# Attention and an MLP mixer on one core: which engine takes the partial sums and the Newton steps, and where the first large block's squares and the weight conversion stand

## The chip, the cores and the metric

The kernel runs on one core of one Trainium2 chip. The metric is the device time of one execution in microseconds. A core has five engines with their own instruction streams: TensorE (PE in the profile, PEld for its weight loads), VectorE (DVE), ScalarE (ACT), GpSimd (POOL) and SyncE (SP), which here issues nearly all DMAs. [...]

## The reference

```python
def _attn_ref(q, k, v, g_q, g_k):               # batch 8, heads 12, seq 448, head_dim 64
    def rmsnorm(x, g):
        rms = np.sqrt(np.mean(x * x, axis=-1, keepdims=True) + 1e-06)
        return x / rms * g
    q_n, k_n = (rmsnorm(q, g_q), rmsnorm(k, g_k))
    scores = 1.0 / np.sqrt(q.shape[-1]) * np.matmul(q_n, k_n.transpose(0, 1, 3, 2))
    scores = scores - np.max(scores, axis=-1, keepdims=True)
    attn = np.exp(scores)
    attn = attn / (np.sum(attn, axis=-1, keepdims=True) + 1e-09)
    return np.matmul(attn, v)
# then, with the heads side by side as x of shape (8, 448, 768):
def _moe_ref(x, w_tok1, w_tok2, w_ch1, w_ch2):  # 448x256, 256x448, 768x1536, 1536x768
    h = np.maximum(x.transpose(0, 2, 1) @ w_tok1, 0.0) @ w_tok2
    u = x + h.transpose(0, 2, 1)
    return u + np.maximum(u @ w_ch1, 0.0) @ w_ch2
```

The mixer's weights arrive as 64-bit floats (an array of 32-bit floats times a 64-bit scalar); everything else is 32-bit.

## The kernel before

**The work.** The 8 images ("b") have 12 heads each. Two heads make a pair (p, 48 in all), and two pairs make a step (t, 24 in all). Attention runs one image ahead of the mixer: while the mixer works on image b, attention works on image b + 1.

**Attention of a step.** For a pair, `square` (ACT, L1259 and L1262) and `reduce` (DVE, L1276) make the sums of squares of q and k; `roots` makes the inverse roots from them by `fold` (ACT, L1284), `guess` (DVE, L1293 and L1298) and three calls of `newton`. A Newton step is three small DVE instructions (L1317 to L1319), or four on GpSimd (L1306 to L1309) for pairs 2 to 11. Roots are made for two pairs at once, under the even pair's number. `scale` (DVE, L349) applies them, and `turn_qk` transposes q and k (from pair 12 on on DVE, L364, with ACT's scaling behind it, L367).

The keys are cut into NK = 7 chunks of 64. `score(t, k)` is 8 matmuls (L387) into two PSUM banks and two exponentials on ACT (L391) into a tile e; `values` multiplies e by v into o_ps (L461). From step 3 on the denominators are made in two stages. `group_sums(t, k)` for k = 1 to 6 adds the seven e tiles into one tile es (L429, 128 x 896): on GpSimd for k = 1 and 2, on DVE for the rest. es is a single buffer. `row_sums` sums es over its rows on PE (d_ps, L441). `denominators` takes the reciprocal of d_ps on DVE (L490, L492, L504) and scales o_ps into uT (L507), which frees the o_ps bank; ps_O has two banks, ps_S (scores and d_ps) four, ps_M (m_ps) two.

**Order.** The order on every engine is the order of emission, and two planners set it. Up to step 8, `att_step` gives four small items per step, and `merge` interleaves them with the mixer's items by their costs. From step BIG = 9 on, `big_step` gives two large blocks per step. It returns what stands ahead of the block, the block, what stands beside it, and what is spread over the units that follow (`place`; for t = 9, which is in the time of image 1's mixer, `merge`). The first block, `first_block`, has the scores 0 and 1, two or three chunks of values of the step before, its row sums and score 2. While step t is computed, the pairs n = 2t + 2 and n + 1 are made ready: for t = 9 these are pairs 20 and 21. Their q and k come by eight DMAs each on SP (L1243).

**The mixer.** For images 1 to 7 the two channel products are computed by a scheme of 7 products of half-size blocks (`ch1`, L880; `ch2`, L937) with sums around them on DVE, ACT and GpSimd (L885 to L919, L946). Image 0 instead uses 36 plain products (`first_stage`, L852), and in its time the weights are converted from 64 to 32 bits, one chunk of 128 x 512 per product. `weight_items` does for item i: the load of chunk i + 2 (SP, L176, two DMAs), the last bit operation of chunk i - 2 (DVE, L281), the first three of chunk i (DVE, L263, L264, L266), ACT's part of chunk i - 1 (L274), the last multiplication of chunk i - 2 into a stage tile (DVE, L308), and the store of chunk i - 3 (SP, L192). `first_items` puts item 19 + k behind product `begins(k)`. With that, the stage tile of product 13 + k is made in the item behind product k + 7 for k from 10 on. The sums of the weights that the 7-product scheme needs are made on GpSimd (L204 to L207); they pass through device memory and are sent from SP (L211) and loaded again (L221, L240, L811).

From image 1 on, the transposed attention output x goes through device memory too: DVE transposes (L742), SP stores (L710) and loads (L717), and then the first token product reads it (L756). The second token product (L764) is added to uT by DVE (L769).

## Time and profile before

| | |
|---|---|
| median of 3 runs | 1330.02 us (1329.81 to 1331.51) |
| the profiled execution | 1331.61 us |
| its span, first to last instruction | 1329.6 us |
| mean granted PE clock | 0.985 |
| PE busy | 1272.4 us (96%) |
| DVE busy | 767.0 us (58%) |
| ACT busy | 372.0 us (28%) |
| POOL busy | 381.0 us (29%) |
| L429 on POOL, 128 x 896 | 42 instructions, 2.09 us median |
| L429 on DVE, 128 x 896 | 84 instructions, 1.09 us median |
| L1317, L1318, L1319 on DVE, 128 x 56 | 54 each, 387, 242 and 241 ns mean |
| L1306 to L1309 on POOL, 112 x 32 | 15 each, 370, 280, 294 and 284 ns mean |

The profile cuts the span into 40 slices of 33.2 us and gives each engine's busy share in a slice in tenths (9 is 90% or more). The list of waits has: engine and line, what it waited for, total us, how often, the longest. The chain of work that ended last goes back from the last instruction, at each step to what released it; its rows are start, duration, what. An idle engine costs nothing unless the chain runs through what it does next. A list of instructions in order of time has start, duration, engine, line, and in brackets the idle time before. Image 0's mixer runs from about 100 to 274 us, image 1's to 448 us, and each later one takes 152 us.

### The profile page before, as it was taken

The page shows a single profiled execution, that of the slowest core. Times are in us where ns is not written, and L with a number is a line of the kernel's source. Part 1 is how long each engine was busy: PE and PEld are TensorE (multiplying, and loading weights), DVE is VectorE, ACT ScalarE, POOL GpSimd, SP SyncE. Part 2 cuts the span into 40 slices and gives each one's busy share as a digit, 9 for nine tenths or more (in the row PEclk, how much of TensorE's full clock was granted, in tenths as well). Part 3 has the DMA queues.
Part 4 walks back from the last instruction along what each step waited for, and adds up shares of the span by engine and source line. Part 5 has one row for each costly group of instructions (what it writes and reads, how often), then busy time and mean ns, then how long its engine had stood idle before and what let it go on. Part 6 is the DMA issues. An engine that isn't in the chain of part 4 may idle for free.

```text
span 1329.6 us, 20169 instructions
## 1 busy us (share of the span) xinstructions
PE 1272.4 (96%) x7408; PEld 936.3 (70%) x7408; DVE 767.0 (58%) x1289; ACT 372.0 (28%) x740; POOL 381.0 (29%) x449
## 2 busy tenths in 40 slices
PE   5989999889997999999999999999999999999997
PEld 3344444346776777896788868886887867797997
DVE  6887689736673366654756367554656457433212
ACT  5553333222331043302332033311433024200100
POOL 1211531255663132221242023321232123311220
PEclk9999999899998999999999999999999999999999
DMA  9656477889879766595757867585766855386554
GB/s 208 170 150 172 115 212 208 195 232 230 229 195 229 156 148 168 142 237 105 168 152 165 207 137 171 141 216 112 185 155 158 223 117 141 113 220 139 175 171 94
DMA packets 502448, 228.05 MB, mean 172 GB/s; under 512 B 374532, under 2 KB 464004, under 8 KB 502340
## 3 DMA queue, kind: packets, MB, share of 16 engines
q1 hardware_dynamic: 489218, 224.83, 68.5%
q10 hardware_dynamic: 12994, 1.84, 0.8%
q8 instruction: 61, 1.00, 0.3%
q14 instruction: 47, 0.39, 0.1%
q0 software_dynamic: 128, 0.00, 0.0%
HBM read 187.07 MB, written 39.52 MB: 170 GB/s over the span
## 4 chain that ended last, share of the span: by engine, by line
PE 82%; DVE 8%; DMA 4%; issue 2%; POOL 1%; SPq 1%; ACT 1%; DVEq 0%; POOLq 0%; ACTq 0%
PE m_ps L880 25%; PE m_ps L937 25%; PE s_ps L387 9%; PE o_ps L461 8%; PE m_ps L764 5%; PE m_ps L756 5%; PE m_ps L852 2%; DMA raw<-in_moe_w_ch_dram 1%; PE d_ps L441 1%; DVE raw L264 1%; DVE raw L281 1%; DVE stage L308 1%; DVE cv_sb L263 1%; PE t_ps L361 1%; DVE ms L1276 1%
## 5 line engine op out<-in xcount | busy, mean ns | idle before, releaser
L937 PE MATMUL m_ps<-hb,unit 128*128 128x224 f32 x1764 | 339.9, 354 | 4.2 <-issue 4.2
L937 PEld LDWEIGHTS m_ps<-hb,unit 128*128 128x128 f32 x1764 | 332.8, 190 | 15.7 <-issue 10.1
L880 PE MATMUL m_ps<-tu,unit 128*128 128x224 f32 x1008 | 201.6, 355 | 0.0
L880 PEld LDWEIGHTS m_ps<-tu,unit 128*128 128x128 f32 x1008 | 189.1, 190 | 14.1 <-issue 7.8
L391 ACT ACTIVATE e<-s_ps 128x448 f32<-128x448 f32 x294 | 138.5, 549 | 175.6 <-PE s_ps L387 173.7
L387 PE MATMUL s_ps<-qkT 64*64 64x448 f32 x1260 | 147.6, 553 | 9.2 <-ACT qkT L367 5.0
L880 PE MATMUL m_ps<-uT,unit 128*128 128x224 f32 x756 | 150.7, 353 | 0.0
L880 PEld LDWEIGHTS m_ps<-uT,unit 128*128 128x128 f32 x756 | 142.6, 190 | 5.0 <-issue 4.3
L461 PE MATMUL o_ps<-e,v 64*64 64x448 f32 x1148 | 131.3, 545 | 0.1
L946 POOL TENSOR_TENSOR uT<-uT,r 128x448 f32<-128x448 f32 (+1 forms) x56 | 49.6, 896 | 256.3 <-DVE r L946 135.5
L885 DVE TENSOR_TENSOR r<-m_ps,r 128x448 f32<-128x448 f32 x63 | 39.2, 622 | 125.3 <-POOL r L885 67.0
L387 PEld LDWEIGHTS s_ps<-qkT 64*64 64x64 f32 x1260 | 46.6, 134 | 77.8 <-issue 59.9
L946 DVE TENSOR_TENSOR uT<-uT,m_ps 128x448 f32<-128x448 f32 (+1 forms) x70 | 33.8, 499 | 108.8 <-PE m_ps L937 105.5
L461 PEld LDWEIGHTS o_ps<-e,v 64*64 64x64 f32 x1148 | 46.7, 135 | 62.8 <-issue 58.3
L429 DVE TENSOR_TENSOR es<-es,e 128x896 f32<-128x896 f32 x72 | 83.9, 1165 | 10.6 <-ACT e L391 8.0
L756 PE MATMUL m_ps<-x,w_sb 112*128 112x384 f32 x256 | 84.8, 488 | 1.0 <-ACT x L736 1.0
L885 POOL TENSOR_TENSOR hb<-r,r 128x448 f32<-128x448 f32 x21 | 24.0, 1141 | 205.3 <-ACT r L901 205.3
L764 PE MATMUL m_ps<-w_sb,h 128*128 128x448 f32 x192 | 78.0, 559 | 4.5 <-DVE uT L769 4.5
L1276 DVE TENSOR_REDUCE ms<-sq 128x28 f32<-128x896 f32 (+2 forms) x45 | 48.7, 1082 | 46.2 <-ACT sq L1262 43.8
L756 PEld LDWEIGHTS m_ps<-x,w_sb 112*128 112x128 f32 x256 | 48.3, 190 | 34.8 <-ACT x L736 1.3
L886 ACT ACTIVATE hb<-hb 128x448 f32<-128x448 f32 x63 | 36.3, 577 | 115.8 <-DVE hb L885 96.9
L764 PEld LDWEIGHTS m_ps<-w_sb,h 128*128 128x128 f32 x192 | 36.6, 196 | 42.4 <-issue 27.4
(124 smaller groups left out, 1444.6 us busy)
## 6 DMA issues: line engine op xcount, KB each, us to landing
unit<-ws SPq DMA_DIRECT2D x294, 384.0 KB, 4.1
raw<-in_moe_w_ch_dram SPq DMA_DIRECT2D x72, 256.0 KB, 3.8
v<-in_v_dram SPq DMA_DIRECT2D x96, 112.0 KB, 3.6
xs<-xt SPq DMA_DIRECT2D x56, 168.0 KB, 4.5
x<-xs SPq DMA_DIRECT2D x14, 672.0 KB, 6.5
out_dram<-turned SPq DMA_DIRECT2D x168, 56.0 KB, 1.9
qk_t<-in_q_dram SPq DMA_DIRECT2D x144, 56.0 KB, 3.3
qk_t<-in_k_dram SPq DMA_DIRECT2D x144, 56.0 KB, 3.9
```

Source lines behind the costliest of these rows:

```text
L387: nc.tensor.matmul(out=pss[i][rows_of(i, a), 0:S], lhsT=qkT[h, 1, k * D:(k + 1) * D], rhs=qkT[h, 0, :], start=True, stop=True)
L391: nc.scalar.activation(out=e[:, i, :], in_=pss[i][:, 0:S], func=AF.Exp)
L429: eng.tensor_tensor(out=es[:], in0=(es if k > 1 else st["e", t, 0])[:], in1=st["e", t, k][:], op=ALU.add)
L461: nc.tensor.matmul(out=st["o", p][a * D:(a + 1) * D, 0:S], lhsT=vt[rows, k * D:(k + 1) * D], rhs=e[rows, :], **kw)
L756: nc.tensor.matmul(out=ps[:, 0:HC], lhsT=w1_sb[0:R, c, jc * P:(jc + 1) * P], rhs=st["x", b, h][0:R, :, c, :], start=(c == 0), stop=(c == N ...
L764: nc.tensor.matmul(out=ps[:, 0:S], lhsT=st["h1", jc][:, cc * P:(cc + 1) * P], rhs=w2_sb[:, jc].rearrange("p c r -> p (c r)"), start=(jc == ...
L880: nc.tensor.matmul(out=ps[:, j * HS:(j + 1) * HS], lhsT=w[:, t, j, :], rhs=m, start=(t == 0), stop=(t == KC - 1))
L885: add = lambda e, o, x, y: e.tensor_tensor(out=o, in0=x, in1=y, op=ALU.add)
L886: relu = lambda x: nc.scalar.activation(out=x, in_=x, func=AF.Relu)
L937: nc.tensor.matmul(out=ps[:, j * HS:(j + 1) * HS], lhsT=st["w"](j, t), rhs=hb[:, HB[what], t, :], start=(t == 0), stop=(t == KF - 1))
L946: add = lambda e, o, x, y: e.tensor_tensor(out=o, in0=x, in1=y, op=ALU.add)
L1276: self.nc.vector.tensor_reduce(out=st["ms", p][:, p % 2, lo:hi], in_=sq[:, lo:hi], axis=AX_X, op=ALU.add)
```

## The change

It has four edits.

1. `group_sums` puts all six additions on DVE.
2. `newton` takes the GpSimd form for pairs from 20 on as well (`far` = 3 * 6 + 2), that is for the roots made in the large blocks.
3. For t = 9 alone, the squares and reductions of pairs 20 and 21 leave their places ahead of, in and beside the first block and are spread behind it, after the denominators and the loads of v and ahead of the roots. For t > 9 the order stays.
4. `begins` puts item 19 + k behind product k + 9 in place of k + 7 for k from 10 on, still at most 29.

```diff
@@ group_sums
-        eng = nc.gpsimd if k < 3 else nc.vector
-        eng.tensor_tensor(out=es[:], in0=(es if k > 1 else st["e", t, 0])[:], in1=st["e", t, k][:], op=ALU.add)
+        nc.vector.tensor_tensor(out=es[:], in0=(es if k > 1 else st["e", t, 0])[:], in1=st["e", t, k][:], op=ALU.add)
@@ big_step, first_block
-            if more:
+            if more and t > BIG:
                 pre.reduce(n, st)
                 pre.square(n + 1, st)
@@ big_step
         if not second:
-            ahead = [item(pre.square, n, st)] if more else []
-            beside = [item(pre.reduce, n + 1, st)] if more else []
+            squares = [item(fn, i, st) for i in (n, n + 1) for fn in (pre.square, pre.reduce)] if more else []
+            ahead, beside = (squares[:1], squares[3:]) if t > BIG else ([], [])
             between = [item(group_sums, t, k) for k in (1, 2) if live]
             ends, roots = ([(0.4, fn) for fn in fns] for fns in (denominators(last), pre.roots(n, st) if more else []))
+            if t == BIG:
+                return ahead, (5.4, first_block), beside, between + ends + [
+                    item(load_v, i, c=0.0) for i in pair] + squares + roots
@@ begins
-        return 2 + -(-k * 14 // 10) if k < 10 else min(k + 7, 29)
+        return 2 + -(-k * 14 // 10) if k < 10 else min(k + 9, 29)
@@ Start.__init__
+        self.far = 3 * self.NPAIR + 2
@@ newton
-        if 1 < p < 2 * self.NPAIR:
+        if 1 < p < 2 * self.NPAIR or p >= self.far:
             nc.gpsimd.tensor_tensor(out=t, in0=y, in1=y, op=ALU.mult)
             nc.gpsimd.tensor_tensor(out=t, in0=t, in1=x, op=ALU.mult)
```

## The prediction

> **What bounds the kernel now.** I read the page first, slice by slice, then who TensorE waited for, then the chain and the engines' order of time around each wait. In the slices TensorE (PE) is 96% busy, and from the fourteenth slice on (430 us) it is at 9 almost everywhere, while VectorE (DVE) falls from 7-9 to 5 and less. So what the change adds to or takes from DVE after 430 us matters only where it makes or removes a hole in PE. The dips lie before: slices 0, 7-8, 12.

> ```profile
> PE   5989999889997999999999999999999999999997
> DVE  6887689736673366654756367554656457433212
> PEclk9999999899998999999999999999999999999999
> ```

> In the first 330 us the list of PE's own waits names the holes: 4.2 us at 96.6 (behind ACT's copy of x), 4.8 us at 235.1 (behind ACT's copy of qkT, which follows DVE's turn L364), 4.5 us at 293.9 (behind DVE L769), 1.7 us at 224.7 (behind ACT L861). The one at 396-429 is in the chain:

> ```profile
> PE s_ps L387 <- ACT qkT L367: 5.0, 2, 4.8
> PE m_ps L764 <- DVE uT L769: 4.5, 1, 4.5
> PE s_ps L387 <- ACT x L736: 4.2, 1, 4.2
> ```
> ```profile
> 407.71 5.34 DMA qk_t<-in_q_dram
> 413.05 0.02 ACT sq L1262
> ...
> 413.88 0.54 ACT e L391
> ...
> 414.46 2.19 PE d_ps L441 x8
> 416.65 1.49 PE s_ps L387 x8
> 418.15 6.91 PE m_ps L937 x32
> ```

> This is the first large block, t = 9. ACT is given the square of pair 20 (L1262) ahead of the block's exponentials. The loads of q and k land at 413, so ACT stands 12.1 us, and PE stands 8.2 us for a score bank that an exponential has to free.

> Last, DVE and GpSimd (POOL) around 91 us, two rows of each in order of time (start, duration):

> ```profile
> 91.44 2.58 DVE L281 SCALAR_TENSOR_TENSOR raw<-raw,cv_sb 128x512 uint32<-128x512 uint32 x1
> 94.06 2.20 DVE L263 TENSOR_SCALAR cv_sb<-raw 128x512 uint32<-128x512 uint32 x1
> ```
> ```profile
> 91.23 2.25 POOL L429 TENSOR_TENSOR es<-e 128x896 f32<-128x896 f32 x1 [29.11 <-ACT e L391]
> 93.55 2.42 POOL L429 TENSOR_TENSOR es<-es,e 128x896 f32<-128x896 f32 x1
> ```

> The same two DVE operations take 0.69 and 0.43 us where POOL is quiet. While POOL adds, DVE stands: 3.7 us here, 2.3 at 141-145, 3.6 at 194-199.

> [...] behind the 8.2 us hole eight d_ps matmuls take 2.19 us, and 0.75 us in the chain elsewhere (128.04); behind the 1.7 us hole nothing slows. [...]

> **The change, part by part.**

> *First large block.* From its start (403.07) to its end (418.15) are 15.1 us. The block of t = 12 takes 1.66 + 2.25 + 1.5 = 5.4 us (640.0 to 645.4); t = 9 has 16 value matmuls for 24, so 4.7. The loss is 10.4 us: 8.2 of standing and 2.2 of slow clock. With the two squares (ACT, 0.95 us each) and reductions (DVE, 1.09 each) behind the denominators, ACT has nothing between 401 and the exponentials. The loads are not moved: pair 20 is there at 413, pair 21 at 418, if SP's queue keeps its distance from PE. What is late next: DVE then waits in reduce(21) until about 419.3, and behind it on DVE are the additions L946 that empty PE's two m_ps banks. PE would be three product units (2.3 us each) past the block, at about 415, and has two banks: a hole of 0 to 2.5 us. The roots follow, but their first user is scale(20) beside the next block, after 468. The v loads (SP) move ahead of squares and roots, whose work is not on SP, so at nothing. I take -10 (-7.5 to -10.4).

> *Partial sums, 42 of them* (21 steps t = 3 to 23, two each). POOL loses the five L429 rows, 88.8 us; DVE gains 42 x 1.09 = 46 us.
> In the large blocks (14, t = 10 to 23) DVE gains 2.2 us just behind the block and loses three Newton steps of 0.65-0.75 us (2.0 to 2.2), and L1293 and L1298, 1.1 and 1.0 us at 650-652 beside a POOL sum, fall to 0.15 and 0.20. DVE thus reaches the second end L507 (656.75) no later than now, with 1.7 us before PE wants its bank (658.47). So nothing is lost. In four of these stages PE now has a hole of 1.04 us (579, 731, 883, 1035), where L946 comes at 578.67 after 8.3 us of DVE work; its new sum is 6.8 us, but a POOL addition L946 can hold the sums back by 1-2 us. I take -2.5 (0 to -4).
> Around 91 us DVE gains 2.2 and loses 3.7 of standing, so reduce(8), ACT's square behind it and the x copy come 1.5 us earlier. The hole of 4.2 becomes 2.7[...]: -3.2, or -1.5 if the clock still falls.

> *Newton steps* for pairs 20 to 46: 14 x 3. DVE loses 126 instructions (54 x (387+242+241) ns for 18 pairs; 14 pairs: 36 us), POOL gains 168. Their shape is not in the trace on POOL; the 112x32 rows give 370+280+294+284 = 1.23 us a step, 56/32 of it is 2.15. I take 1.7, 5 us for three, against 2.2 on DVE. Behind them on DVE waits the scale beside the second block. There PE has 6.2 us of scores and values that need no fresh DVE work, so up to 6 us of lateness are covered: nothing, and up to +1 us a block if POOL's own hb sums (L912, L919) come between.

> *Conversion.* Twelve items (k = 10 to 21) go two products later (the last, one): each has five DVE operations (2.87 us), one ACT (L274, 0.7), two weight loads and one store on SP. Nothing leaves; DVE is busy without a break from 199 to 255 us but for some 2 us of loads. They move behind the sums, roots, scales and turns of pairs 12 and 13. I added DVE's operations in the new order. k = 10 and 11 no longer fill the time until the exponentials of 203 us, so some 4 us are idle there. Then 31 us of work lead to turn L364 of pair 13 at about 235.5, with the earlier start about 233, for 238-239 now. The holes at 224.7 and 235.1 (1.7, and 7.4 with its slow clock) shrink by 4 to 6. The rest of DVE's list is the same sum, 56 us from 203: the last turn of x (L742) ends at 258 to 261, for 262.1 now. Stage tile 35 is ready at 255-258; PE wants it near 265.
> But this gain has to pass the hole at 293.9. SP issues almost without a break from 262 to 281 (x stores, weight sums, y stores, x load), starting behind L742; the sums' load, POOL's sums and L862, DVE's turns and L769 hang on that chain:

> ```profile
> 276.57 5.71 DMA raw<-ws
> ...
> 285.93 2.19 POOL uT L862 x2
> 288.14 0.65 DVE turned L973
> ...
> 297.75 0.59 DVE uT L769
> 298.39 1.86 PE m_ps L764 x2
> ```

> So only what L742 gains (1 to 4 us) and part of the gain at 96 us come through[...]. For the first image, sums and conversion together, I take -5 (-9 to +1).

> **Sum.** -10 - 5 - 2.5 = -17.5. The profiled execution took 1331.61 us (span 1329.6 and 2.0 around it), 1.6 above the median of 1330.02. So 1314.1 on its scale, 1312.5 on the median's.

> **The rivals.**
> *Only the large block pays.* The chain behind L742 gives back all of the first image, and POOL's additions hold the new sums so that the four small holes stay: 1330.0 - 10 = 1320. For it: SP has no slack at 262-281. Against: POOL's load there falls too.
> *The wait moves instead of going.* At t = 9 the loads of pairs 20 and 21 land when they land; reduce(21) on DVE holds PE's banks for some 8 us, and the first image gives nothing: 1329, the same. For it: SP is busy with these loads until 415. Against: three units and two banks lie between.
> *Slower.* The two sums stand ahead of the denominators on DVE in each of the 14 large first blocks, and the value banks or m_ps are freed late. The place is L507 before PE's L461; the slack is 1.7 us. It decides from 17.5/14 = 1.25 us a block; at 2 us past that slack it is 28 - 17.5 = +10.5: 1340. For it: DVE does sit between both banks. Against: what DVE loses in the same stretch is as long.
> The change does what it says: it can fail only where scale waits for POOL, which is priced above.

> **How the numbers follow.** A measurement of this kernel tells 0.2% (2.7 us) from no change. Forecast 0.55 (1305 to 1317), only the large block 0.28 (1317 to 1326), the wait moves 0.07, slower 0.10. The first two are faster: with a little of each case's edge, 0.85; same 0.05; slower 0.10. The range takes both, 1305 to 1326.

> **What would show it.** Right: PE without a hole at t = 9 (d_ps x8 near 0.75 us), ACT's wait for qk_t off PE's path, no 2 us DVE rows at 91 and 194, L364 of pair 13 near 233, slices 7 and 12 of PE at 9, POOL near 363 us (381 - 88.8 + 42 x 1.7). Wrong: PE waiting for reduce(21) or L946 at 410-420; a longer hole before L764; PE waiting for a stage tile at products 30 to 35; or new holes of over 1 us behind each first block.

## The result and the profile after

The changed kernel takes a median of **1318.46 us** (4 runs, 1316.73 to 1319.78) against 1330.76 us for the kernel before in the same comparison (4 runs, 1329.81 to 1332.71): a ratio of 0.9905, interval 0.9888 to 0.9922, 12.3 us faster. The forecast was 17.5 us. The profiled execution took 1318.47 us with a span of 1316.7, so the two profiled spans differ by 12.9 us.

Line numbers moved by one to three: the sums L429 are now L428, d_ps L440, o_ps L460, the x turn L744, the x stores L712, the x load L719, the token products L758 and L766, `first_stage` L854 with its ACT copies L863, `ch2` L939, its sums L948, `square` L1265, `reduce` L1279. In the variants a and c they are one higher again from the sums on.

First the slices of the page, as before: busy tenths of PE and DVE, and the granted clock.

```profile
PE   5989999889999999999999999999999999999997
DVE  6887688927774366644666267644666356433212
PEclk9998999999999999999999999999999999999999
```

Counted from 0, slice 12 of PE is at 9 now and the clock's dip there is gone, as is the one in slice 7 (slice 3 is at 8 instead). Slices 7 and 8 of PE are still at 8. The list of PE's own waits (total us, times, longest) says why:

```profile
PE m_ps L758 <- DMA x<-xs: 4.4, 1, 4.4
PE s_ps L387 <- ACT qkT L367: 4.2, 2, 4.0
PE s_ps L387 <- ACT x L738: 2.8, 1, 2.8
PE m_ps L766 <- ACT h L761: 2.5, 1, 2.5
```

The first and the last of these were not in the list before. The first large block, t = 9, in PE's instructions in order of time:

```profile
402.25 1.68 PE L460 MATMUL o_ps<-e,v 64*64 64x448 f32 x16
403.75 0.93 PE L440 MATMUL d_ps<-es,one_c 64*64 64x448 f32 x8
404.50 0.93 PE L387 MATMUL s_ps<-qkT 64*64 64x448 f32 x8
405.36 16.16 PE L939 MATMUL m_ps<-hb,unit 128*128 128x224 f32 x84
422.13 4.81 PE L939 MATMUL m_ps<-hb,unit 128*128 128x224 f32 x24 [0.61 <-DVE uT L948]
```

No idle time stands in brackets before the d_ps matmuls, and eight of them take 0.93 us (the next starts 0.75 us later) where they took 2.19. Last, DVE around 91 us, the same two operations that had stood for 2.58 and 2.20 us:

```profile
91.37 0.68 DVE L281 SCALAR_TENSOR_TENSOR raw<-raw,cv_sb 128x512 uint32<-128x512 uint32 x1
92.09 0.43 DVE L263 TENSOR_SCALAR cv_sb<-raw 128x512 uint32<-128x512 uint32 x1
```

To see where the 12.9 us are, I cut the span at four starts on PE's own order of work: the product unit that starts at 86 us (L758 x8), the scores behind the third group of image 1's second token product, image 2's first token product, and image 6's first. Lengths between such starts do not depend on where a trace begins. "Later period" is the mean of the next four images. The stretches are those of one profiled execution each.

| kernel | median us, ratio [interval] | first image: 86 us to the scores | rest of image 1's mixer | later period |
|---|---|---|---|---|
| before | 1330.76 | 217.75 | 144.44 | 152.08 |
| after | 1318.46, 0.9905 [0.9888, 0.9922] | 217.40 | 136.39 | 151.01 |
| a: block alone | 1329.28, 0.9977 [0.9968, 0.9987] | 218.07 | 141.40 | 152.07 |
| b: conversion back | 1315.42, 0.9879 [0.9863, 0.9896] | 213.29 | 136.32 | 151.01 |
| c: sums back | 1320.83, 0.9915 [0.9899, 0.9932] | 218.58 | 139.61 | 150.76 |
| d: Newton back | 1323.65, 0.9935 [0.9918, 0.9951] | 217.12 | 138.49 | 151.85 |
| e: x turns first | 1321.43, 0.9917 [0.9900, 0.9934] | 218.53 | 138.18 | 151.01 |
| g: b, four items later | 1316.83, 0.9883 [0.9865, 0.9901] | 214.80 | 138.21 | 151.01 |
| h: b, five sums last | 1314.80, 0.9873 [0.9856, 0.9889] | 207.72 | 140.92 | 151.01 |
| i: g and h | 1315.58, 0.9881 [0.9865, 0.9898] | 211.73 | 138.11 | 151.01 |

From before to after: the first image 0.35 us, the rest of image 1 8.05, four periods 4.28 (4 x 1.07); 0.2 more lie ahead of 86 us and behind image 6.

Two things limit how finely the table can be read. The variants were timed in two later comparisons, in which the kernel before took 1332.28 us (a to d) and 1332.03 (e to i) for 1330.76 here. So it is the ratios that compare across them: against the kernel after, they put c 1.3 us higher, d 4.0 and e 1.6, and b 3.5 us lower, g 2.9, h 4.3 and i 3.2. The differences of medians below differ from these by about 1.3 us. And after a hole PE's granted clock is at half for 0, 3.41 or 6.83 us in the traces of before and after (10.24 behind the 8.2 us hole), and holes of one length did not cost the same in every record (last section). Fourteen value matmuls (L460) took 3.36 us from start to start at a clock of 0.50 in after (from 102.09 us), 1.71 at 1.00 in b (from 100.87).

### The profile page after: what moved, and what is told of

It is laid out like the page before. It is cut to its first block, busy times and chain, and to the rows that moved or that the text cites. A ratio compares the mean times of both kernels' runs of the same rounds, so it can differ in the third digit from the quotient of the medians.

```text
span 1316.7 us, 20214 instructions
## 1 busy us (share of the span) xinstructions
PE 1269.7 (96%) x7408; PEld 933.5 (71%) x7408; DVE 763.8 (58%) x1205; ACT 372.6 (28%) x740; POOL 355.0 (27%) x575
## 4 chain that ended last, share of the span: by engine, by line
PE 75%; DMA 2%; DVE 1%; SPq 1%; POOL 0%; issue 0%; ACT 0%; DVEq 0%; POOLq 0%; ACTq 0%
PE m_ps L882 25%; PE m_ps L939 25%; PE s_ps L387 7%; PE o_ps L460 7%; PE m_ps L758 5%; PE m_ps L766 5%; PE d_ps L440 1%; DMA unit<-ws 1%; DMA x<-xs 0%; DMA qk_t<-in_k_dram 0%; DMA ws<-raw 0%; SPq L702 0%; DVE es L428 0%; DVE ms L1279 0%; DVE nt L1321 0%
## 5 line engine op out<-in xcount | busy, mean ns | idle before, releaser
L939 PE MATMUL m_ps<-hb,unit 128*128 128x224 f32 x1764 | 339.6, 353 | 2.2 <-DMA unit<-ws 1.5
L939 PEld LDWEIGHTS m_ps<-hb,unit 128*128 128x128 f32 x1764 | 332.2, 190 | 13.3 <-issue 10.9
L391 ACT ACTIVATE e<-s_ps 128x448 f32<-128x448 f32 x294 | 138.4, 549 | 188.2 <-PE s_ps L387 179.4
L387 PE MATMUL s_ps<-qkT 64*64 64x448 f32 x1260 | 145.4, 549 | 7.0 <-ACT qkT L367 4.2
L460 PE MATMUL o_ps<-e,v 64*64 64x448 f32 x1148 | 132.7, 547 | 0.1
L428 DVE TENSOR_TENSOR es<-es,e 128x896 f32<-128x896 f32 x90 | 109.7, 1219 | 19.6 <-ACT e L391 14.7
L948 POOL TENSOR_TENSOR uT<-uT,r 128x448 f32<-128x448 f32 (+1 forms) x56 | 57.8, 1041 | 231.4 <-DVE r L948 143.6
L887 DVE TENSOR_TENSOR r<-m_ps,r 128x448 f32<-128x448 f32 x63 | 39.2, 622 | 112.2 <-PE m_ps L882 59.0
L387 PEld LDWEIGHTS s_ps<-qkT 64*64 64x64 f32 x1260 | 45.6, 133 | 75.7 <-issue 59.4
L948 DVE TENSOR_TENSOR uT<-uT,m_ps 128x448 f32<-128x448 f32 (+1 forms) x70 | 33.8, 499 | 109.7 <-PE m_ps L939 109.7
L460 PEld LDWEIGHTS o_ps<-e,v 64*64 64x64 f32 x1148 | 46.4, 135 | 63.9 <-issue 60.3
L758 PE MATMUL m_ps<-x,w_sb 112*128 112x384 f32 x256 | 86.4, 494 | 5.5 <-DMA x<-xs 4.4
L887 POOL TENSOR_TENSOR hb<-r,r 128x448 f32<-128x448 f32 x21 | 24.4, 1163 | 241.5 <-ACT r L903 241.5
L766 PE MATMUL m_ps<-w_sb,h 128*128 128x448 f32 x192 | 75.5, 544 | 4.0 <-ACT h L761 2.5
L758 PEld LDWEIGHTS m_ps<-x,w_sb 112*128 112x128 f32 x256 | 49.1, 193 | 40.8 <-issue 8.5
L1279 DVE TENSOR_REDUCE ms<-sq 128x28 f32<-128x896 f32 (+2 forms) x45 | 48.6, 1082 | 33.2 <-ACT sq L1265 30.5
L766 PEld LDWEIGHTS m_ps<-w_sb,h 128*128 128x128 f32 x192 | 35.4, 190 | 40.7 <-issue 26.4
```

What stands on the lines that cost most here:

```text
L387: nc.tensor.matmul(out=pss[i][rows_of(i, a), 0:S], lhsT=qkT[h, 1, k * D:(k + 1) * D], rhs=qkT[h, 0, :], start=True, stop=True)
L391: nc.scalar.activation(out=e[:, i, :], in_=pss[i][:, 0:S], func=AF.Exp)
L428: nc.vector.tensor_tensor(out=es[:], in0=(es if k > 1 else st["e", t, 0])[:], in1=st["e", t, k][:], op=ALU.add)
L460: nc.tensor.matmul(out=st["o", p][a * D:(a + 1) * D, 0:S], lhsT=vt[rows, k * D:(k + 1) * D], rhs=e[rows, :], **kw)
L758: nc.tensor.matmul(out=ps[:, 0:HC], lhsT=w1_sb[0:R, c, jc * P:(jc + 1) * P], rhs=st["x", b, h][0:R, :, c, :], start=(c == 0), stop=(c == N ...
L766: nc.tensor.matmul(out=ps[:, 0:S], lhsT=st["h1", jc][:, cc * P:(cc + 1) * P], rhs=w2_sb[:, jc].rearrange("p c r -> p (c r)"), start=(jc == ...
```

## The experiments

Theory A, from the prediction: each edit is worth its own stretch, and the worths add. Rival: the edits share queues, so that one is worth little without another.

**a. The large block alone.** Before, with edit 3 only.

```diff
-            if more:
+            if more and t > BIG:
                 pre.reduce(n, st)
...
+            if t == BIG:
+                return ahead, (5.4, first_block), beside, between + ends + [
+                    item(load_v, i, c=0.0) for i in pair] + squares + roots
```

> Only the first large block's edit; sums, Newton steps and conversion as before. Theory (the four edits act in different stretches and add up): PE reaches the scores behind the third token product (304.07 us before) at the same time, the stretch from there to image 2's first token product (448.51 before, 440.04 after) shortens by 8 us as in the changed kernel, the four holes of 1.04 us stay: about 1322.5. Rival (the block's gain leans on GpSimd being freed of the sums, since the last weight sums queue behind them): a longer hole at 420-430 behind the weight loads, half of the gain lost: about 1326.

Measured: 1329.28 us (10 runs) against 1332.28 (13 runs), 3.0 us, which is less than the theory and the rival had. The hole of 8.2 us in the block is gone here too, and others stand behind it. The chain of waits in that stretch (pieces left out are marked):

```profile
409.54 5.78 DMA unit<-ws
...
417.35 0.42 SPq L1247
...
417.87 3.76 DMA ws<-raw
421.63 0.95 ACT sq L1266
...
427.38 0.62 DVE uT L949
...
430.12 4.37 DMA unit<-ws
```

PE has holes of 0.99 and 0.82 us behind `unit` loads, 2.97 behind L949 and 1.77 behind `unit` again. SP is late with all of these loads. Two `unit` loads are issued 10.4 us behind the start of the products that follow the block (416.40 for 405.95), and 7.4 us after all four edits (412.79 for 405.36). The last load of pair 21 (L1247) is issued at 417.35, after all four edits at 413.74. Its square, for which the chain names the store `ws<-raw` that was issued just behind that load, starts at 421.62 for 417.95, and `reduce` is late with it. Then nine Newton instructions follow on DVE (L1321 to L1323), until 427.29. All this stands ahead of L949, which frees PE's bank.

SP's lateness starts 22 us earlier, at the first store of x: there SP waits 8.7 us for DVE's turn L745, and 5.1 us in the kernel after. DVE in order of time, first here, then in the kernel after:

```profile
377.84 1.42 DVE L1297 SCALAR_TENSOR_TENSOR ms<-ms,half 128x56 f32<-128x56 f32 x1
379.30 2.11 DVE L1302 TENSOR_SCALAR rs<-ms 128x56 int32<-128x56 int32 x1
...
392.95 1.65 DVE L745 STREAM_TRANSPOSE xt<-uT 128x448 f32<-128x448 f32 x3
```
```profile
377.26 0.22 DVE L1296 SCALAR_TENSOR_TENSOR ms<-ms,half 128x56 f32<-128x56 f32 x1
377.51 0.33 DVE L1301 TENSOR_SCALAR rs<-ms 128x56 int32<-128x56 int32 x1
...
388.74 1.65 DVE L744 STREAM_TRANSPOSE xt<-uT 128x448 f32<-128x448 f32 x3
```

Beside the two rows that are long here POOL makes its two sums of t = 8 (377.10 and 379.26 us, 2.08 and 2.09 long). The turn ends at 394.60 for 390.39 us, 4.2 us later, while PE is only 0.6 us later at the block's first scores (401.28 for 400.69). So DVE's standing beside POOL's sums reaches PE some 40 us later, through SP's queue.

So the rival holds: **alone, the edit turns most of its hole into other waits**. Theory A's addition is wrong. Of this stretch's 8.05 us the edit brings 3.0 by itself; 3.2 more come when the sums leave POOL (c) and 2.1 when Newton leaves DVE (d), together 8.3. A run with those edits and without the block's was not made.

**c. The sums back on GpSimd.** After, with edit 1 undone. The theory laid the four 1.04 us holes of the later periods to DVE's standing beside POOL's sums (L1298 took 1.98 us beside a sum of 2.07 at 572.9 us before, 0.17 to 0.20 where POOL was quiet).

```diff
-        nc.vector.tensor_tensor(out=es[:], ...)
+        eng = nc.gpsimd if k < 3 else nc.vector
+        eng.tensor_tensor(out=es[:], ...)
```

> The changed kernel with the sums k = 1 and 2 on GpSimd again. Theory [...]: they return, +4.2 us, and the hole at 96 grows by 1.4 without reaching the end: about 1322.5. Rival (the Newton steps' leaving VectorE closed the holes): no hole returns, 1318.5.

Measured: 1320.83 us, 2.4 above after and between theory and rival; the intervals of the two ratios overlap. The four 1.04 us holes of the later periods do not come back: 150.76 us each, 0.25 shorter than after. In the rest of image 1 it is 3.2 us longer (139.61 for 136.39), with five holes behind `unit` loads (4.2 us together, 1.5 after), and SP's wait for the turn of x is 8.7 us, both as in a (in d, with the sums on DVE, it is 5.1 us). Neither theory nor rival had this.

**d. Newton back on DVE.** After, with edit 2 undone. The theory (0 to +1 us) was that of c: DVE only stood beside POOL's sums.

```diff
-        if 1 < p < 2 * self.NPAIR or p >= self.far:
+        if 1 < p < 2 * self.NPAIR:
```

> The changed kernel with all later Newton steps on VectorE again. [...] 0 to +1 us, 1318.5 to 1319.5. Rival (VectorE's sum of work behind the third large block decides: 6.8 us with the Newton steps gone, 8.9 with them, against 8.3 before): the four holes return at 1.0 to 1.6 us each, 1322.5 to 1325.

Measured: 1323.65 us, 5.2 above after (the two intervals overlap a little) and within the rival's range. PE's instructions in order of time, behind the first large block and in the first later period, and the latter in the kernel before:

```profile
423.81 4.81 PE L939 MATMUL m_ps<-hb,unit 128*128 128x224 f32 x24 [2.49 <-DVE uT L948]
...
573.12 20.67 PE L939 MATMUL m_ps<-hb,unit 128*128 128x224 f32 x108 [0.64 <-PE m_ps L939]
```
```profile
579.91 5.35 PE L937 MATMUL m_ps<-hb,unit 128*128 128x224 f32 x27 [1.04 <-issue]
```

The hole behind L948 is 2.49 us in place of 0.61, since the Newton steps stand on DVE between `reduce` and L948. And a hole of 0.64 us stands in each of four later periods, which are 0.84 us longer each than in the kernel after; the rival had 1.0 to 1.6. The 5.2 us stand against 2.1 (138.49 less 136.39) and 4 x 0.84, 5.5 in all. With c this says who made the four holes: with the POOL sums and without DVE's Newton there is none, with DVE's Newton and the sums on DVE too there is one. **What DVE has to do between the block and L948 makes them, Newton above all; GpSimd's additions alone do not.**

**b. The conversion back.** After, with edit 4 undone.

```diff
-        return 2 + -(-k * 14 // 10) if k < 10 else min(k + 9, 29)
+        return 2 + -(-k * 14 // 10) if k < 10 else min(k + 7, 29)
```

> The changed kernel with the conversion where it was (k + 7 for k + 9). Theory (the later conversion only moves the first image's loss: from the hole at 235 to the wait for x at 278): the hole before the scores at 232 is longer again (about 5 us and slow clock), the last turn of x ends near 260 in place of 265.4, the wait for x is gone or under 1 us, and PE is at the scores behind the third token product 0 to 2 us earlier than 303.65: 1316.5 to 1318.5. Rival (the later conversion is worth its 3 to 6 us and without it the first image is worse): 1321 to 1324.

Measured: 1315.42 us, 3.0 below after (the two intervals still overlap a little) and below the theory's range, and the first image is 4.1 us shorter (213.29 for 217.40). Two rows of PE in order of time:

```profile
99.20 1.57 PE L387 MATMUL s_ps<-qkT 64*64 64x448 f32 x10 [2.81 <-ACT x L738]
...
296.23 3.27 PE L766 MATMUL m_ps<-w_sb,h 128*128 128x448 f32 x8 [1.89 <-DVE uT L771]
```

At 99 us the hole is as long as after, 2.81 us, but here the clock held: 1.57 us for ten score matmuls, 2.50 after. The edit does not account for that: d, whose code in image 0 is that of the kernel after, held it as well (1.57 us), and its first image is 217.12 us all the same. b leads by 2.8 us at 103 and 1.0 us at 140, where other waits take part of it. The rest, 3.2 us, arises between 140 us and the scores (160.05 us here, 163.21 after): PE does not wait for x at 283, and of the hole of 4.5 us before (and the slow clock behind it) 1.4 and 1.9 us remain. So without the POOL sums the first image is 4.5 us shorter than before, some 1 us of it by the clock at 99 us, and **the conversion edit took it back.** By itself (c, in the first image) it gains nothing: 218.58 for 217.75.

**e. The x turns ahead of the last conversions.** After b the question was whether DVE's late turn or SP's queue holds x. So: after, with image 1's last x turns emitted ahead of the last three conversion items; SP's order of the stores among themselves stays.

```diff
-            last = x_items(1, 1) + merge(last, direct + sums[:5], turns(b, y_order(b)[2:4]))
+            att += x_items(1, 1)
+            last = merge(last, direct + sums[:5], turns(b, y_order(b)[2:4]))
```

> The changed kernel with image 1's last three x transposes (L744) emitted ahead of the last three conversion items; SP's order is as in the changed kernel. Theory (what makes x late is SP's queue: the stores of the last stage tiles, L192, wait there for the late conversions, and the x stores L712 stand behind them): L744 ends some 6 us earlier, near 259, the x load does not move by over 1 us, PE's wait of 4.4 us for x stays: 1317.5 to 1319. Rival (VectorE's order alone makes x late): x lands 4 to 6 us earlier, the wait goes, 1313 to 1316.

First DVE, then SP's issues, in order of time:

```profile
256.19 1.69 DVE L744 STREAM_TRANSPOSE xt<-uT 128x448 f32<-128x448 f32 x3
```
```profile
256.76 8.01 SPq L192 DMA_DIRECT2D ws<-stage  x4
264.82 0.50 SPq L712 DMA_DIRECT2D xs<-xt  x1
...
276.52 0.44 SPq L719 DMA_DIRECT2D x<-xs  x1
```

The turn ends 7.6 us earlier than after (257.9 for 265.5), the store of x 0.7 us (264.82 for 265.53) and its load 1.0 (276.52 for 277.51); a hole of 3.22 us behind x stays, 4.44 after. The median, 1321.43 us, is 3.0 above after and above the theory's range, though the intervals overlap: 1.1 us in the first image, and 1.8 behind it, where a hole behind a `unit` load is 1.99 us and a slow clock follows it (0.58 and 0.56 in the next 4 us). SP stands ahead of x's first store in four stores of stage tiles (L192); of these 8.0 us, 6.2 are waits for L308, the last multiplication of the conversion. So the earlier turn did not help: the stores that waited these 6.2 us for late conversions held back x's store behind them in SP's queue. The last conversions stand behind the turn on DVE here, which lengthens these waits (3.8 us in the kernel after). A run with x's stores ahead of the stage stores was not made.

**g, h, i. Can the hole at 238 and those at 293 go as well?** All three start from b. g puts four items later, by two products (k = 15 to 17) and one (k = 18). h puts the first five sums of the weights behind the last six products of image 0. i does both.

```diff
-        return ... min(k + 7, 29)
+        return ... min(k + (9 if 15 <= k <= 17 else 8 if k == 18 else 7), 29)
```
```diff
-            last = x_items(1, 1) + merge(last, direct + sums[:5], turns(b, y_order(b)[2:4]))
+            last = x_items(1, 1) + merge(last, direct, turns(b, y_order(b)[2:4])) + sums[:5]
```

> The kernel b_conv_back (conversion at k + 7) with the items k = 15 to 17 two products later and k = 18 one later. Theory (VectorE had nothing to do in the 5 us before the exponentials of 204 us because items 10 and 11 were taken away; without that idle time the last turn of x stays near 261): pair 13's turn L364 comes near 229 for 237, PE's holes at 225 and 239 with their slow clock (8.8 us) go, but the chain over SP, the weight sums and L864 ends when it did, so PE waits at 280 to 296 for it: 0 to 3 us faster than b_conv_back, 1312.5 to 1315.5. Rival (any later conversion costs the end): 1318.

> The kernel b_conv_back with the first five weight-sum items behind image 0's last six products, so that GpSimd's L864 does not stand behind sums that wait for a load. Theory (L864, VectorE's turns, the partial sums, the reduction and ACT's relu of the token product hang on that load): both holes at 292 to 296 (1.4 and 1.9 us) go: 1311.5 to 1313. Rival (the weight sums themselves are due soon after, and PE waits for its units instead): new waits for unit tiles after 305, no gain, 1315 to 1318.

> g_three_later and h_sums_last together. Theory: with L864 off the sums' load, PE keeps more of the 8.8 us gained at 225 to 240; it is then held by the x load (SP's queue), which leaves 2 to 5 us: 1307 to 1311. Rival (the x load holds it all): as h_sums_last, 1311.5 to 1313.

g: 1316.83 us, above the theory's range. The hole at 238 (4.84 us in b) is 0.95, and a new one of 7.71 stands at 255, behind ACT's copy L863. ACT in order of time:

```profile
246.04 0.72 ACT L274 ACTIVATE cv_sb<-cv_sb,expo_c 128x512 uint32<-128x512 uint32 x1 [2.13 <-DVE cv_sb L266]
253.40 0.72 ACT L274 ACTIVATE cv_sb<-cv_sb,expo_c 128x512 uint32<-128x512 uint32 x1 [6.64 <-DVE cv_sb L266]
254.03 0.95 ACT L863 COPY r<-m_ps 128x448 f32<-128x448 f32 x2
```

ACT stood 6.64 us in its part of a late conversion, and behind it the copies that empty PE's banks: **the items that were moved for DVE's sake now hold ACT.** i has the same hole, 7.40 us, and takes 1315.58 us, more than theory and rival had.

h: 1314.80 us, between theory and rival and the lowest median of all, though not told apart from b by these runs. The holes at 293 and 296 are gone and the first image is 5.6 us shorter than b's. 1.4 us of that lies behind the hole of 4.84 us at 238, as long in both: from its end to the end of the 80 products of L854 are 33.3 us in h and 34.7 in b. Of the 5.6 us, 4.6 are lost in the rest of image 1 (140.92 for 136.32), where PE waits 1.7 us for L887 at 334 and 2.2 for `unit` at 419, with a slow clock behind that (0.61 and 0.54 in the next 4 us; 60 products take 13.27 us for 11.59 in b); the sums that were put off are late for these users. I have not attributed the remainder. b and h both beat the kernel before. h is probably better than the change as given, too: its interval, 0.9856 to 0.9889, only just touches 0.9888 to 0.9922.

## Why the prediction came out as it did

The direction and the largest part were right; the sum was 5 us too good, and 1318.46 lies just outside the 1305 to 1317 that the forecast case had for its own, in those of the rival "only the large block pays" (1317 to 1326). That rival had half of the mechanism: the chain behind the x turn did give back the first image, but the four small holes did go. That the first two terms together came out at 12.3 us for 12.5 is luck: one was 2 us too large, the other 1.8 too small.

**First large block, -10: measured -8.05, mechanism right.** The hole and the slow clock went as worked out: from the block's first scores to the products behind it are 4.67 us (4.7 predicted) for 15.08. Reduce(21) runs from 418.94 to 420.02 (predicted until 419.3), and the hole behind it is 0.61 us (0 to 2.5). Missing from the term was a hole of 1.52 us behind a `unit` load at 428: SP's queue was not followed past the block. But that the block would bring this **by its own edit** was wrong: a gave 3.04 in that stretch. The rest needs POOL free of the sums (c) and DVE free of Newton (d). The prediction put Newton at nothing and did not see that it stands in front of the freeing of PE's banks just where reduce(21) is late. And it counted DVE's standing beside POOL's sums only where PE waited for DVE soon after; at 377 us it comes to PE through the turn of x and SP's queue. The condition that it named, "if SP's queue keeps its distance from PE", was the one that failed in a.

**Partial sums in the later blocks, -2.5: measured -4.28, and for another reason.** The four holes went, and no new one came, so the size was near. The step that fails is the cause: Newton's leaving DVE removed them (c and d). DVE did stand beside POOL's sums here as well (L1298 of the kernel before took 1.98 us at 725 us, beside a sum of 2.07, and at 718 in c; in d, with the sums on DVE, 0.19 at 720), but in these later blocks those waits had cover.

**First image, -5: measured -0.35; this is the term that failed.** It had three steps.
At 96 us the hole became 2.81 us (2.7 predicted), and no DVE row stands at 2 us there any more. The -3.2 put down for it also took it that the clock would hold there. That was the author's estimate: in the kernel before it held behind a hole of 1.69 us (1.00 at 226.4 to 228.4 us) and fell behind the 4.2 us one (0.50). Behind the hole of 2.8 us it held in three records of seven (last section). And of what was gained at 103 us (0.7 us after, 3.5 in b) nothing was left after, and 0.8 in b, at 140 us, where PE waits for a load of v in b (0.49 us). A gain was counted at its hole and not followed to the next marker.
The turn L364 of pair 13 started at 235.38 (233 predicted, before 238.04), and the holes at 224 and 235 shrank from 6.5 to 4.0 us, with a slow clock behind the latter still (0.50 from 239.3 to 241.3 us).
The last turn of x was to end at 258 to 261; it ended at 265.5: the 56 us of DVE work from 203 on took 61.6, from 203.88. DVE in order of time, near the end of it:

```profile
252.76 1.26 DVE L266 TENSOR_SCALAR cv_sb<-raw 128x512 uint32<-128x512 uint32 x1
253.92 1.64 DVE L308 SCALAR_TENSOR_TENSOR stage<-raw 128x512 f32<-128x512 f32 x1
...
263.82 1.68 DVE L744 STREAM_TRANSPOSE xt<-uT 128x448 f32<-128x448 f32 x3
```

L266 takes 0.43 and L308 0.70 us where POOL is quiet; longer rows like these add up to 2.9 us between 252 and 264 us, and DVE stood another 1.4 us for loads at 237 and 241. POOL's L864 and then its sums of the weights (L204 to L207) run from 252.09 on and now meet the late conversions. I had moved the conversions on DVE and ACT and named their stores on SP, but priced neither this meeting nor the stores that now stand ahead of x. The chain of waits shows what follows:

```profile
271.06 1.79 SPq L712
...
277.51 5.31 DMA x<-xs
282.95 7.04 PE m_ps L758 x16
```

The x load is issued 3.6 us later than in the kernel before (277.51 for 273.92):

```profile
273.92 0.44 SPq L717 DMA_DIRECT2D x<-xs  x1
```

PE stands 4.44 us for it, and the slow clock takes 1.6 more (7.04 for 5.43). In experiment e a turn that ended 7.6 us earlier brought the load forward by 1.0 us alone, with the late stage stores still ahead of it on SP. The prediction had written "SP has no slack at 262-281" as evidence for the rival and did not draw it through its own sum.

**What held:** the slower rival did not occur (no hole behind the later first blocks), and POOL is busy for 355.0 us, 363 predicted: a 128 x 56 Newton step takes 1.12 us there, 1.45 from start to start, for 1.7 assumed. One reading of the slices was off without consequence: behind 430 us DVE was at 3 to 7 tenths until the last slices, not at 5 and less.

## What to carry to other kernels

A step that is moved takes all of its queue places along: follow its DMA issue and its part on each other engine past everything that now stands behind them, since here the gain on DVE was lost on SP (PE stood 4.44 us for x) and, in g, on ACT (7.71 us behind L863). An engine's delay can reach the bottleneck through another engine's queue and much later, as in a, where 4 us on DVE came to PE some 40 us on. Count a removed hole as a gain only if nothing else is due within it: a took out 8.2 us and got 3.0, and the other edits that looked like nothing (Newton) or like something else (the sums) were what let the rest through. Where several edits are made at once, take each out of the whole as well as putting it in alone; here the whole without one edit (b) is probably the better kernel.

## What the runs showed of the hardware

PE's clock does not follow from the length of a hole alone. In seven records the same hole at 97 to 99 us is 2.81 to 2.86 us long: behind it ten score matmuls took 2.50 or 2.51 us in four (after, e, g, i) and 1.57 in three (b, d, h). The granted clock just behind it, first after, then b:

```profile
99.31:101.31 2.00, 2.00 (x10) 0.50 0.05 13
```
```profile
99.20:101.20 2.00, 2.00 (x18) 1.00 0.08 24
```

Shorter holes were followed by a slow clock as well: of those behind a `unit` load at 419 to 430 us, the clock fell in e, g and h (1.92 to 2.17 us; the 60 products behind took 13.27 us), and held in after, b, c, d and i (1.52 to 1.85 us; 11.59 in b, c, d and i). Granted clock (the number behind PE's count) in stretches behind the hole, first e, then i:

```profile
429.58:431.58 2.00, 2.00 (x6) 0.58 0.95 356
431.58:433.58 2.00, 2.00 (x7) 0.56 1.17 335
```
```profile
424.53:426.53 2.00, 2.00 (x11) 1.00 1.03 355
```

But a hole of 2.49 us in d, at 421 us, left the clock at 1.00, so no single bound on the length fits.

The traces of before and after also show when the granted clock changed. Between 84 and 1195 us these are all its stretches at half, with the time that PE was idle in the 3.41 us just ahead of each:

| kernel | half clock from, us | for, us | PE idle in the 3.41 us ahead |
|---|---|---|---|
| before | 98.60 | 6.83 | 2.03 |
| before | 238.55 | 6.83 | 3.41 |
| before | 296.57 | 6.83 | 2.69 |
| before | 409.21 | 10.24 | 2.98 |
| after | 98.54 | 6.83 | 2.04 |
| after | 238.49 | 3.41 | 2.23 |
| after | 282.86 | 3.41 | 3.41 |

These are readings of two traces and one hole of a third. Why the changes lie where they do, and what counts as idle inside the chip, no run here shows.
